# Feed forward in units of two, four, four, four and two tiles, and another order of the steps

## The chip, the core and the metric

The kernel runs on one core of a Trainium2 chip. The metric is the device time of one execution in microseconds (us), the median of three runs. A core has five engines with queues of their own: TensorE (PE in the profile) for matmuls, with its weight loads shown apart (PEld), VectorE (DVE), ScalarE (ACT), GpSimd (POOL) and SyncE (SP), which issues nearly all DMAs here.

## The reference, cut to what matters

One transformer block over 2048 rows of 640 bf16 numbers: linear attention with 32 heads of 20, then a feed forward layer of width 1728.

```python
x = A_x                                    # 1 x 2048 x 640
h = x + attention(layernorm(x), wqkv, w_phi, wo)
out = h + silu(layernorm(h) @ w1) @ w2     # w1: 640 x 1728, w2: 1728 x 640

# attention, for each head, on q, k, v of 20 columns:
phi(a) = concat(softmax(a @ w_phi), softmax(-(a @ w_phi)))     # 40 features
kv, z  = sum over rows of phi(k)^T v,  sum over rows of phi(k)
o      = phi(q) @ kv / (phi(q) @ z + 1e-6)
attention = concat of the heads' o @ wo
```

The sums kv and z run over all 2048 rows, so no query can be used before the last key has been added.

## The kernel before, in words

The rows are cut into 16 tiles of 128 (T = 16). The kernel is a dictionary of small steps, each a Python function that emits a few instructions, and a string ORDER that lists the steps' names. The program is emitted in exactly that order, so ORDER fixes the order on every engine's queue: an engine runs its own instructions in the order of the string and waits at each for its inputs and for its buffer. A second table, ON, says which engine takes some of the copies and normalisations.

The steps, with a tile's number t, and the line at which the profile shows them:

- `WKc`, `WVc`, `Xa`, `loadi`, `wph`: loads of weights and input on SP (L163, L166, L490). `X2` brings tiles 2 and 3. `load0` is wo, `load1` to `load5` the five row blocks of w1, `load6` to `load9` four parts of w2, `load10` and `load11` its last 64 rows.
- `wk`, `wke`, `fk`, `fke` (TensorE L292, L316, copies L309, L325): w_phi folded into the key weights at the start; `wq` (a transposing DMA, L388), `fq`, `fqe` (L400, L406) the same for the query weights. `own`, `phq`, `phi_a`, `phi_b`, `ones`, `pad`, `mask`, `eqp` prepare constants.
- `st t` (VectorE L434, L435), `rs t` (GpSimd L443, L446 or ScalarE L440), `xn t` (VectorE or GpSimd L450): the first layernorm. `xt t` transposes the tile: tiles 0 to 3 on TensorE (L457, copied by `x t`, L477), the others by a DMA that SP issues (L479).
- `K t`, `V t` (TensorE L498; tile 0's V in five parts, L510), `ex t` (ScalarE L539), `su t` (VectorE L543), `rk t` (ScalarE L551, L552), `sc t` (VectorE L556), `ve t` (ScalarE L560), `kv t` (TensorE L575): keys' features, values and their sums. `bd0`, `bd1` (VectorE L584, L586) turn the sums into block diagonal weights.
- `Q t` (TensorE L522), `qe t` (ScalarE L639), `qs t` (VectorE L643), `qr t` (VectorE L651, L653, L661), `qt t` (a transposing DMA, L667): queries' features.
- `D t` (TensorE L692), `E t0`, `E t1` (VectorE L704, L705), `ot t` (transposing DMA, L716), `G t0`, `G t1` (TensorE L725), `ga t0`, `ga t1` (VectorE L732): numerator and denominator, division, output projection, residual.
- `ls t` (L434, L435), `lr t` (GpSimd L443, L446), `hn t` (VectorE L450), `ht t` (transposing DMA, L752): the second layernorm, transposed into the buffer HnT.
- Feed forward by units of tiles, a unit named by its first tile a: `ua.f` (TensorE L815) multiplies column chunks of w1 from f on (128 columns each, 13 whole chunks) with the unit's HnT, into one PSUM bank of 512 numbers; `sa.f` (ScalarE L835) takes silu of the bank into shT. The last 64 columns of w1 go the other way round (`ua.L`, L826; `sa.L`, L841; `lta`, a transposing DMA, L845). `d t0`, `d t1` (TensorE L853, L856) multiply with w2, `oa t0`, `oa t1` (VectorE L862) add the residual, `out t` (L867) stores.

Before the change the units are tile 0, tile 1, and then pairs (2, 3) to (14, 15). A unit of n tiles has a moving operand of 128 n columns, so 128 in the first two units and 256 in the others. A piece, one bank, is four chunks in a unit of one tile and two in a unit of two. A unit's first `u` needs HnT of all its tiles. HnT has four buffers (NHN) of two tiles' size, shT three (NSH).

PSUM has eight banks. At first they are used as three pairs, with two banks for the sums over keys; from the step `halves` on as a ring of eight single banks, taken in turn, so that each use waits for the emptying of the one eight before it.

Of the kernel before, what the change touches and what calls it, by code (L numbers as in the profile page):

```python
# [15 lines left out]


ORDER = """
warm0 warm1 warm2 warm3 warm4 warm5 warm6 warm7 warm8 warm9 warm10 warm11 warm12 warm13 warm14 own pad0
X0 st0 phi_a WK0 WK1 wk0 warm15 warm16 warm17 WK2 wk1 rs0 xn0 WK3 WK4 xt0 warm18 wk2 X1 wke0 ones5 WV0  # L20
WV1 WV2 phi_b wk3 wke1 wke3 wk4 fk3 x0 WV3 wke2 WV4 fk2 wke4 st1 ones3 X2 fk1 fk3e fk4 rs1 fk1e fk2e X4
xn1 V0.0 st2 fk4e wph0 mask fk0 mask0 wph1 rs2 X8 V0.1 st3 xn2 V0.2 ones0 st4 fk0e phq xt1 ones1 x1 K0
ex0 rs3 V0.3 xn3 V1 zeros xt2 ve1 st6 x2 rs4 xn4 wq2 load10 rs6 xt4 K1 st5 su0 rs5 ex1 xt3 V2 ve2 K2 x3
ex2 rk0 wq0 V0.4 K3 fq2 ex3 xn5 xn6 V3 ve0 st8 fq2e su1 ones4 st7 ve3 wq3 ones2 rk1 sc0 V4 su2 ve4 rs7
xt5 fq0 xn7 load8 fq0e sc1 kv0 st9 su3 K4 xt6 wq4 fq3 rs8 ex4 rk2 st11 sc2 fq3e wq1 V5 rs9 kv1 ve5 st10
K5 rk3 K6 ex5 kv2 sc3 V6 ex6 xn8 fq1 ve6 xt7 xn9 xt8 rs10 pad1 kv3 su4 rk4 rs11 K7 su5 fq1e ex7 xn10 V7
fq4 rk5 ve7 wq5 sc4 kv4 su6 rk6 V8 sc5 st12 st14 st13 K8 kv5 xn11 fq4e ve8 ex8 xt9 xt10 ones6 fq5 fq5e
sc6 su7 K9 Q0 ex9 ones7 V9 load11 xt11 rk7 load7 qe0 kv6 rs12 K10 su9 sc7 xn12 su8 rs13 K11 load9 load1
rk9 ve9 rs14 xn14 st15 ex10 sc9 kv7 xn13 rk8 sc8 xt12 Q1 V10 ex11 qe1 ve10 su11 kv8 kv9 xt13 rk11 qs0
rs15 eqp K12 ex12 V11 su10 xn15 rk10 ve11 V13 K13 sc11 su12 ve13 xt14 sc10 V12 load5 ex13 kv10 qr0 kv11  # L30
su13 K14 V14 qs1 load2 xt15 qr1 rk13 ve12 load6 K15 load3 ex14 ve14 rk12 Q2 ex15 V15 su14 sc13 rk14 qe2
qt0 su15 Q3 sc14 Q4 sc12 rk15 ve15 kv12 kv13 qe3 sc15 mask1 kv14 qs2 qs3 Q5 qe4 qr2 kv15 qt1 qr3 bd1 bd0
Q6 load0 qe5 Q7 Q8 qe6 halves qt2 D0 qe7 qs4 qt3 Q9 E00 qe8 qe9 E01 D1 Q11 E10 E11 Q10 qr4 qe11 qe10 D2
qs5 ot0 Q13 qe13 G00 E20 G01 ot1 E21 ga00 ga01 ls0 D3 qt4 Q12 Q14 ot2 G10 qe12 E30 lr0 load4 hn0 E31 qs6
qr6 Q15 G11 G20 qe14 qr5 qe15 G21 ht0 ot3 ga11 ga10 u0.L ls1 lr1 ga20 u0.4 s0.L qt5 lt0 D4 E40 u0.12 hn1
u0.0 ga21 s0.0 u0.8 qs9 s0.12 ht1 qt6 G30 G31 s0.4 ga30 s0.8 d00 ga31 ls2 d01 E41 D5 u1.L u1.0 lr2 ls3
u1.4 oa00 s1.0 s1.L oa01 u1.8 u1.12 ot4 hn2 E50 s1.12 ht2 G40 lr3 hn3 ht3 E51 D6 qs7 s1.4 E60 G41 ga40
ot5 qr9 u2.0 s1.8 u2.10 E61 u2.2 u2.L qr7 ga41 s2.0 qs8 ls4 u2.6 u2.12 G50 s2.10 lt1 s2.2 lr4 G51 qr8
hn4 s2.L ga51 u2.4 s2.4 ot6 lt2 u2.8 ga50 ls5 s2.8 lr5 qs10 hn5 qs12 qt7 s2.6 qr10 d11 d10 s2.12 qt8 ht4
G60 ht5 oa10 out0 D7 d31 ga60 qs15 d30 E70 qt9 d20 E71 oa11 oa20 out1 G61 ot7 u4.0 oa30 D8 oa31 u4.8  # L40
s4.0 qr12 d21 qt10 u4.L ga61 s4.8 E80 E81 s4.L ls6 u4.12 oa21 qs11 qr15 s4.12 u4.2 D9 u4.6 s4.2 lr6 u4.4
G70 u4.10 E90 s4.4 lt4 hn6 G71 s4.10 ot8 E91 out2 G80 s4.6 ot9 G81 ga71 ga81 ga70 d50 d41 G90 ls7 qs13
lr7 ht6 hn7 D10 oa50 ga80 ls8 ht7 lr8 E100 out3 hn8 d40 G91 d51 qr11 oa40 E101 oa41 u6.0 ga91 ga90 u6.12
oa51 qr13 ot10 u6.10 u6.6 u6.L s6.L s6.0 s6.6 u6.2 u6.4 qt11 lt6 s6.12 ls9 s6.10 u6.8 G100 lr9 s6.4 s6.2
ht8 s6.8 hn9 ht9 out5 D11 G101 qs14 d60 u8.L out4 s8.L d61 ga101 E110 ga100 u8.0 qt12 qr14 u8.10 s8.0
oa60 E111 ot11 qt15 ls10 d70 oa61 G110 lt8 D12 oa70 G111 E120 u8.4 qt13 lr10 s8.10 u8.8 u8.6 E121 qt14
u8.12 s8.8 ga110 D13 s8.4 ga111 ls11 E130 lr11 hn10 u8.2 s8.12 s8.6 d71 oa71 hn11 ot12 out7 ht11 s8.2
E131 d90 out6 d80 G120 d91 G121 oa80 ga120 ht10 ot13 u10.0 oa90 oa91 ga121 s10.0 D14 u10.4 E140 u10.L
u10.12 E141 G130 u10.8 s10.4 D15 ga130 s10.12 s10.8 ls12 u10.2 E150 u10.10 lr12 s10.L G131 E151 hn12
ot14 u10.6 G140 d81 ga131 s10.2 lt10 G141 out9 oa81 out8 ls13 s10.10 s10.6 ht12 ga140 lr13 d110 ga141  # L50
hn13 d101 d100 ls14 ht13 d111 oa110 u12.0 u12.2 u12.10 oa100 ot15 oa111 u12.4 oa101 u12.L u12.12 s12.0
s12.2 s12.4 u12.8 lr14 s12.10 u12.6 hn14 s12.L G150 s12.8 s12.6 s12.12 G151 ht14 ga150 lt12 out10 out11
d120 ga151 ls15 lr15 d121 oa120 hn15 ht15 d130 oa121 out12 u14.L oa130 u14.0 s14.L lt14 u14.2 s14.0
u14.4 s14.2 u14.6 s14.4 u14.8 s14.6 u14.10 s14.8 u14.12 s14.10 d131 s14.12 d140 oa131 out13 d141 oa140
d150 oa141 out14 d151 oa150 out150 d152 oa151 out151 oa152 out152
""".split()

# [2 lines left out]
def kernel(  # L60
# [82 lines left out]

    ON = dict(
        rs0="ACT", xn0="DVE", wke0="DVE", wke1="DVE", wke3="ACT", x0="DVE", wke2="DVE", wke4="DVE",
        fk3e="ACT", rs1="POOL", fk1e="DVE", fk2e="ACT", xn1="DVE", fk4e="ACT", rs2="POOL", xn2="DVE",
        fk0e="ACT", x1="ACT", rs3="ACT", xn3="DVE", x2="ACT", rs4="ACT", xn4="DVE", rs6="POOL", rs5="POOL",
        x3="ACT", xn5="POOL", xn6="POOL", fq2e="ACT", rs7="POOL", xn7="POOL", fq0e="ACT", rs8="ACT",
        fq3e="ACT", rs9="ACT", xn8="POOL", xn9="POOL", rs10="ACT", rs11="POOL", fq1e="ACT", xn10="POOL",
        xn11="POOL", fq4e="ACT", fq5e="ACT", rs12="POOL", xn12="POOL", rs13="POOL", rs14="POOL", xn14="DVE",  # L150
        xn13="POOL", rs15="ACT", xn15="POOL",
    )


# [614 lines left out]
    def ffn_step(at):  # L769

        u = unit(int(at))
        steps = [f"u{u[0]}.{p[0]}" for p in pieces(u)]
        downs = [f"d{t}{g}" for t in range(*u) for g in range(2)]
        k = 2 * (at - u[0]) / (u[1] - u[0])
        return steps[int(k * len(steps))] if k < 1 else downs[int((k - 1) * len(downs))]
# [70 lines left out]

    def ffn_down(u, t, g):
        k, n = t - u[0], (u[1] - u[0]) * P
        ps = ps_of["d", t, g] = ps_half()
        a, b = groups(t)[g]  # L850
        for fc in range(FC - 1):
            at = fc * n + k * P
            nc.tensor.matmul(  # L853
                ps[:, 0 : b - a], shT[u][:, at : at + P], w2_sb[:, fc, a:b], start=(fc == 0), stop=False,
            )
# [74 lines left out]
```

## Time and profile before

| what | us |
|---|---|
| median of three runs (238.47, 239.26, 239.35) | 239.26 |
| the profiled execution | 239.66 |
| its span, from the first instruction to the last | 237.9 |
| TensorE busy in the span | 229.7 |
| VectorE busy | 170.5 |
| ScalarE busy | 104.4 |
| GpSimd busy | 55.2 |
| first matmul of D0, from the span's start | 76.1 |
| first matmul of the last step with matmuls (d152) | 233.1 |

The profile is of one execution, and all times below count from the start of its span. A matmul's row is longer than its share of the stream, since matmuls overlap in the array; what a matmul costs is read from one start to the next. TensorE's granted clock was 0.997 of full speed over the span, and full from 4.3 us on.

### The profile page before, as it was taken

What the parts mean: (1) busy time and instruction counts of PE and PEld (TensorE: products, weight loads), DVE (VectorE), ACT (ScalarE), POOL (GpSimd) and SP (SyncE); (2) the same over time, 40 slices, a digit from 0 to 9 for tenths busy, and PEclk for the clock granted to TensorE, in tenths of its full rate; (3) what the DMA queues carried; (4) which work ended last, traced back from release to release, by engine and by line L of the source; (5) the groups of instructions that cost most, each with busy time, mean ns of one, the idle gap of its engine ahead of it and who ended that gap; (6) DMA issues with size and microseconds to landing.
All of it is one profiled execution on the core that took longest, in us unless ns stands there. A gap on an engine that the chain in (4) does not pass through costs nothing.

```text
span 237.9 us, 5586 instructions
## 1 busy us (share of the span) xinstructions
PE 229.7 (97%) x2253; PEld 180.4 (76%) x2253; DVE 170.5 (72%) x355; ACT 104.4 (44%) x222; POOL 55.2 (23%) x99
## 2 busy tenths in 40 slices
PE   7999999989999999999999999999999999999993
...
DVE  4799999999999999979997869854535634242021
...
PEclk9999999999999999999999999999999999999998
...
GB/s 170 295 282 125 126 156 62 283 179 87 230 184 64 145 155 102 110 98 39 149 118 116 62 56 56 96 167 85 165 51 90 36 54 83 30 61 63 0 46 38
DMA packets 67472, 26.87 MB, mean 113 GB/s; under 512 B 60407, under 2 KB 66423, under 8 KB 67319
## 3 DMA queue, kind: packets, MB, share of 16 engines
...
q14 instruction: 8, 0.07, 0.1%
...
## 4 chain that ended last, share of the span: by engine, by line
PE 75%; POOL 9%; DMA 7%; DVE 3%; ACT 2%; issue 1%; SPq 1%; POOLq 0%; DVEq 0%
PE banks L815 23%; PE banks L853 23%; PE banks L725 9%; PE banks L522 8%; POOL xn L450 7%; PE banks L498 5%; DMA X<-in_A_x_dram 2%; PE banks L692 2%; DMA OT<-O 2%; PE banks L856 2%; DVE st L434 2%; DMA Wk<-in_A_wqkv_dram 2%; DMA w_sb<-in_B_w_dram 1%; PE banks L575 1%; PE banks L826 1%
## 5 line engine op out<-in xcount | busy, mean ns | idle before, releaser
L835 ACT ACTIVATE shT<-banks 128x512 bf16<-128x512 f32 (+2 forms) x57 | 30.1, 560 | 75.3 <-PE banks L815 75.2
L853 PE MATMUL banks<-w_sb,shT 128*128 128x320 bf16 (+2 forms) x429 | 61.4, 295 | 0.0
L815 PE MATMUL banks<-HnT,w_sb 128*128 128x256 bf16 (+1 forms) x585 | 61.0, 261 | 0.0
L815 PEld LDWEIGHTS <-w_sb 128*128 128x128 bf16 x585 | 51.0, 98 | 5.5
L853 PEld LDWEIGHTS <-shT 128*128 128x128 bf16 x429 | 41.1, 98 | 14.9
L443 POOL TENSOR_SCALAR rs<-mv 128x1 f32<-128x1 f32 x25 | 5.7, 228 | 149.8 <-DVE mv L435 149.8
L862 DVE TENSOR_TENSOR o_t<-banks,X 128x320 bf16<-128x320 f32 (+2 forms) x33 | 15.5, 476 | 33.3 <-PE banks L856 28.0
L498 PEld LDWEIGHTS <-XnT 128*128 128x128 bf16 x310 | 29.4, 98 | 11.8 <-DMA XnT<-xn 1.2
L434 DVE BATCH_NORM_STATS2 st<-X 128x6 f32<-128x320 bf16 x64 | 27.9, 478 | 5.1 <-DMA X<-in_A_x_dram 4.9
L450 POOL TENSOR_SCALAR xn<-X,mv,rs 128x640 bf16<-128x640 bf16 x10 | 25.3, 2532 | 5.5 <-ACT rs L441 5.2
L725 PE MATMUL banks<-wo_sb,OT 128*128 128x320 bf16 x160 | 25.6, 299 | 0.2 <-DMA OT<-O 0.2
L732 DVE TENSOR_TENSOR X<-banks,X 128x320 bf16<-128x320 f32 x32 | 14.8, 481 | 15.2 <-PE banks L725 15.2
L498 PE MATMUL banks<-Wfk,XnT 128*128 128x320 bf16 x160 | 24.2, 299 | 0.8 <-DMA XnT<-xn 0.8
L643 DVE TENSOR_REDUCE Sq<-EQ 128x66 f32<-128x1320 bf16 x16 | 24.1, 1512 | 0.0
L522 PE MATMUL banks<-Wfq,XnT 128*128 128x360 bf16 (+2 forms) x160 | 23.6, 299 | 0.0
L639 ACT ACTIVATE EQ<-banks 128x660 bf16<-128x660 f32 (+2 forms) x46 | 21.8, 558 | 3.9 <-PE banks L522 3.7
L543 DVE TENSOR_REDUCE Sk<-EK 128x64 f32<-128x1280 bf16 x16 | 23.3, 1468 | 0.0
L498 PE MATMUL banks<-Wv,XnT 128*128 128x320 bf16 x150 | 22.5, 299 | 0.0
L539 ACT ACTIVATE EK<-banks 128x640 bf16<-128x640 f32 x32 | 20.7, 698 | 3.2 <-PE banks L498 2.2
L522 PEld LDWEIGHTS <-XnT 128*128 128x128 bf16 x160 | 15.1, 97 | 6.1
L725 PEld LDWEIGHTS <-OT 128*128 128x128 bf16 x160 | 15.3, 98 | 5.8 <-DMA OT<-O 0.5
L705 DVE TENSOR_TENSOR O<-banks,Rd 128x360 bf16<-128x360 f32 (+1 forms) x32 | 15.7, 491 | 1.1
...
## 6 DMA issues: line engine op xcount, KB each, us to landing
...
```

The source lines that it names most:

```text
L434: nc.vector.bn_stats(st[:, i, :], X[:, t, i * HD : (i + 1) * HD])
L450: eng.tensor_scalar(out=xn_[t][:], in0=X[:, t, :], scalar1=mv_.pop(t)[:, 0:1], scalar2=rs_.pop(t)[:], op0=ALU.subtract, op1=ALU.mult,)
L498: nc.tensor.matmul(ps[:, g, 0:HD], XnT[:, c, t * P : (t + 1) * P], W[:, c, g * HD : (g + 1) * HD], start=(c == 0), stop=(c == C - 1),)
L522: nc.tensor.matmul(ps[:, 0 : e - a], XnT[:, c, t * P : (t + 1) * P], Wfq[:, c, a:e], start=(c == 0), stop=(c == C - 1),)
L539: nc.scalar.activation(E5[:, :, :, b, :], p4, AF.Exp, scale=sign)
L543: nc.vector.tensor_reduce(sk[t][:], ek[t][:, 0 : H * HF].rearrange("p (q f) -> p q f", f=DH), axis=AX.X, op=ALU.add)
L639: nc.scalar.activation(features(t, a, b)[:, :, :, i], p4, AF.Exp, scale=sign)
L643: nc.vector.tensor_reduce(sq[t][:], EQ[0][:, t, :, 0:FCH].rearrange("p c (q f) -> p c q f", f=DH), axis=AX.X, op=ALU.add)
L725: nc.tensor.matmul(ps[:, 0:HD], ot[t][:, c, :], wo_sb[:, c, g * HD : (g + 1) * HD], start=(c == 0), stop=(c == C - 1),)
L815: nc.tensor.matmul(ps[:, at : at + n], w1_sb[:, c, fc * P : fc * P + P], HnT[u][:, c, 0:n], start=(c == 0), stop=(c == C - 1),)
L835: nc.scalar.activation(shT[u][:, f0 * n : f1 * n], ps_of.pop(("u", u, f0))[:, 0 : (f1 - f0) * n], AF.Silu)
L853: nc.tensor.matmul(ps[:, 0 : b - a], shT[u][:, at : at + P], w2_sb[:, fc, a:b], start=(fc == 0), stop=False,)
```

## The change

The units become (0, 1), (2 to 5), (6 to 9), (10 to 13) and (14, 15). The moving operand has 256 columns in the first and the last unit and 512 in the three between; a piece there is one chunk. HnT and shT hold four tiles, with three and two buffers. `ua.L` does each tile once (before, a unit of one tile did it twice to fill the 128 rows), and its transpose and w2's last rows follow the tile's number in the unit. An unused helper (`ffn_step`) goes, and there are twenty matmuls ahead of the kernel's work instead of nineteen (WARM).

ORDER is another one from its start up to the last unit's steps; it holds the same steps, but for the units' pieces and `warm19`. ON gives the normalisations of tiles 4 and 14 (`xn4`, `xn14`) to GpSimd, which then has twelve of them instead of ten, and moves `wke0`, `wke1`, `x0` from VectorE to ScalarE, `rs0`, `rs3`, `rs9`, `rs10` to GpSimd and `rs6`, `rs7`, `rs11` to ScalarE. Between the last `kv` and `D0` stands one Q instead of three, so that ten Q follow D0 instead of seven. SP issues the twelve loads ahead of `X2` in the same order as before; `load9` now stands between `xt7` and `xt8`, `load10` between `lt0` and `qt7`.

```diff
-    WARM = 19
+    WARM = 20
...
-    NHN = 4
-    NSH = 3
-    SINGLE = 2
+    NHN = 3
+    NSH = 2
...
-        xn11="POOL", fq4e="ACT", fq5e="ACT", rs12="POOL", xn12="POOL", rs13="POOL", rs14="POOL", xn14="DVE",
-        xn13="POOL", rs15="ACT", xn15="POOL",
+        wke0="ACT", rs0="POOL", wke1="ACT", xn0="DVE", wke3="ACT", wke2="DVE", fk3e="ACT", rs1="POOL",
+        x0="ACT", wke4="DVE", xn1="DVE", fk2e="ACT", fk1e="DVE", fk0e="ACT", fk4e="ACT", x1="ACT",
+        rs2="POOL", xn2="DVE", rs3="POOL", x2="ACT", xn3="DVE", rs4="ACT", x3="ACT", rs6="ACT", xn4="POOL",
...
-    UNITS = [(t, t + 1) for t in range(SINGLE)] + [(t, t + 2) for t in range(SINGLE, T, 2)]
+    UNITS = [(0, 2)] + [(t, t + 4) for t in range(2, T - 2, 4)] + [(T - 2, T)]
...
-            HnT[u] = persist.tile([P, C, 2 * P], BF16, name="HnT", bufs=NHN)
+            HnT[u] = persist.tile([P, C, 4 * P], BF16, name="HnT", bufs=NHN)
...
-        m = 2 if u[1] - u[0] == 2 else 4
+        m = 4 // (u[1] - u[0])
...
-        for j in range(2):
+        for j in range(n // P):
...
-                    ps[:, j * FL : (j + 1) * FL], HnT[u][:, c, (j * P) % n : (j * P) % n + P],
+                    ps[:, j * FL : (j + 1) * FL], HnT[u][:, c, j * P : (j + 1) * P],
...
-            shT[u] = pools["late"].tile([P, 2 * (FC - 1) * P], BF16, name="shT", bufs=NSH)
+            shT[u] = pools["late"].tile([P, 4 * (FC - 1) * P], BF16, name="shT", bufs=NSH)
...
-        nc.tensor.matmul(ps[:, 0 : b - a], shT_l[u][:, 0], w2_last[:, k, a:b], start=False, stop=True)
+        nc.tensor.matmul(ps[:, 0 : b - a], shT_l[u][:, k // 2], w2_last[:, k % 2, a:b], start=False, stop=True)
```

Of ORDER, the stretch around D0 and the one around the first units, before and after:

```diff
-qt0 su15 Q3 sc14 Q4 sc12 rk15 ve15 kv12 kv13 qe3 sc15 mask1 kv14 qs2 qs3 Q5 qe4 qr2 kv15 qt1 qr3 bd1 bd0
-Q6 load0 qe5 Q7 Q8 qe6 halves qt2 D0 qe7 qs4 qt3 Q9 E00 qe8 qe9 E01 D1 Q11 E10 E11 Q10 qr4 qe11 qe10 D2
...
+V15 qe2 kv12 Q5 rk14 su15 qs2 sc14 qe3 rk15 kv13 sc15 kv14 ve15 qt0 kv15 qe5 load1 qr2 Q7 halves bd0 bd1
+qt1 qs3 D0 E00 Q4 E01 D1 qe7 qe4 qr3 Q9 E10 qe9 Q6 qt2 load3 Q8 E11 qe6 Q10 D2 ot0 G00 qe8 qs5 pad0 qs4
+qr4 E20 qt3 G01 E21 ot1 Q11 ga01 qr5 ga00 qe10 Q14 qt4 G10 qe11 D3 ls0 ot2 qt5 ga10 E30 E31 G11 qe14 Q12
+ga11 D4 lr0 Q13 hn0 ls1 G20 qe12 E40 qe13 ot3 lr1 hn1 ga20 Q15 G21 ht0 qe15 E41 G30 D5 G31 ht1 u0.0 u0.2
...
+lr5 s0.12 d01 ga41 d00 hn5 ls4 lr4 qs8 ht2 hn4 qs10 qr8 ot6 oa00 d11 oa01 ht5 ht4 D7 d10 G60 E70 oa10
+out0 G61 u2.6 E71 qt8 u2.0 oa11 qr10 u2.9 u2.11 ga61 s2.0 s2.6 ga60 s2.9 s2.11 qs9 qr9 u2.2 D8 u2.L ot7
```

More of the change, by code (lines that the diff above doesn't have):

```diff
@@ L18 @@
 ORDER = """
[L19 to L28, printed above, removed]
@@ L34 @@
[L34 to L38, printed above, removed]
@@ L44 @@
[L44 to L53, printed above, removed]
@@ L54 @@
-u14.4 s14.2 u14.6 s14.4 u14.8 s14.6 u14.10 s14.8 u14.12 s14.10 d131 s14.12 d140 oa131 out13 d141 oa140
+warm0 warm1 warm2 warm3 warm4 warm5 warm6 warm7 warm8 warm9 warm10 warm11 warm12 warm13 warm14 phi_b
+phi_a ones1 X0 WK0 WK1 WK2 st0 wk0 warm15 warm16 warm17 warm18 WK3 wk1 warm19 WK4 wke0 rs0 X1 WV0 WV1
+WV2 wke1 wk2 wk3 xn0 wke3 fk3 WV3 xt0 wke2 WV4 fk2 fk3e X2 st1 wk4 wph1 X4 rs1 fk1 wph0 x0 wke4 xn1 fk0
+fk2e wq2 zeros fk1e fk4 V0.0 V0.1 xt1 ones6 fk0e own fk4e st2 x1 rs2 st3 K0 xn2 ex0 X8 K1 st4 V0.2 ones3
@@ new lines @@
+rs3 V0.3 wq3 xt2 ex1 x2 xn3 su0 V1 xt3 K2 rs4 ve1 x3 rk0 V0.4 K3 st6 st5 V3 st7 ones0 ex2 sc0 phq fq2
+rs6 xn4 ex3 V2 ve3 fq3 ve0 su1 xt4 st8 fq2e load11 rs7 ve2 rs5 wq0 xn5 kv0 xt5 su2 xn6 rk1 V4 sc1 K4
+ones2 fq3e fq0 ve4 kv1 wq1 V5 rs8 ex4 xt6 wq4 K5 xn7 su3 rk2 xt7 st10 xn8 fq0e fq1 ve5 sc2 st9 rk3 rs9
+kv2 K6 ex5 su4 sc3 fq1e load9 st11 K7 xn9 kv3 st12 st13 rs10 rk4 sc4 ones4 ex6 ex7 xt8 V6 xn10 xt9 wq5
+fq4 su5 V7 ve6 fq4e V8 ve7 ones7 su6 ones5 rk5 rs12 st15 rs11 V9 rs13 xn11 ve8 sc5 K8 load2 kv4 ve9 rk6
@@ new lines @@
+fq5 ex8 fq5e xt10 su7 rk7 sc6 su8 xn13 K9 st14 kv5 Q0 load6 xt11 rs15 K10 sc7 load4 ex9 su9 xn12 qe0 kv6
+Q1 kv7 xt13 mask eqp rs14 ex10 xn14 rk8 qs0 sc8 rk9 su10 V10 K11 qe1 xt12 V11 ve10 sc9 ex11 rk10 su11
+V13 qs1 ve11 rk11 kv8 sc11 load0 K12 sc10 qr0 xn15 K13 ve13 kv9 xt14 ex12 load7 K14 ex13 su12 su13 mask0
+kv10 V14 kv11 xt15 load5 rk12 ex14 sc12 rk13 ve14 V12 mask1 K15 su14 sc13 load8 ve12 Q2 Q3 pad1 qr1 ex15
+V15 qe2 kv12 Q5 rk14 su15 qs2 sc14 qe3 rk15 kv13 sc15 kv14 ve15 qt0 kv15 qe5 load1 qr2 Q7 halves bd0 bd1
@@ new lines @@
+qt1 qs3 D0 E00 Q4 E01 D1 qe7 qe4 qr3 Q9 E10 qe9 Q6 qt2 load3 Q8 E11 qe6 Q10 D2 ot0 G00 qe8 qs5 pad0 qs4
+qr4 E20 qt3 G01 E21 ot1 Q11 ga01 qr5 ga00 qe10 Q14 qt4 G10 qe11 D3 ls0 ot2 qt5 ga10 E30 E31 G11 qe14 Q12
+ga11 D4 lr0 Q13 hn0 ls1 G20 qe12 E40 qe13 ot3 lr1 hn1 ga20 Q15 G21 ht0 qe15 E41 G30 D5 G31 ht1 u0.0 u0.2
+qs6 u0.4 E50 ot4 ga21 ga30 u0.10 E51 u0.L ot5 ga31 qr6 s0.0 G40 s0.L u0.8 ls3 qt6 qs7 G50 qr7 s0.2 u0.6
+ls2 lt0 ga50 s0.10 s0.4 lr3 s0.6 G51 ga40 lr2 u0.12 G41 D6 load10 hn3 qt7 ga51 hn2 ls5 E60 s0.8 ht3 E61
@@ new lines @@
+lr8 ht6 ot11 ga90 d50 d40 qs15 ls9 oa30 lr9 ht7 oa21 hn8 oa31 G100 hn9 out2 qs14 oa40 d51 G101 ht9 ht8
+G110 out3 G111 ga110 ga111 d41 ga100 oa50 u6.L D12 oa51 u6.0 qr14 s6.L ga101 E120 u6.11 qt13 u6.1 s6.0
+s6.1 oa41 E121 u6.8 D13 u6.12 ls10 E130 ls11 lr11 s6.12 E131 u6.2 s6.11 ot12 qt14 u6.10 u6.5 out4 u6.9
+s6.8 u6.6 u6.3 ot13 qr15 u6.4 s6.5 s6.2 s6.3 s6.9 qt15 G120 s6.4 u6.7 s6.10 lr10 G121 lt6 G130 ga120
+s6.6 G131 D14 ga121 s6.7 hn11 ga131 ga130 ht11 out5 ls13 d60 hn10 ls12 lr13 lr12 d61 oa60 d70 E140 d71
```

42 lines of the change are left out of this document (19 added, 23 removed).

## The prediction

> **What bounds the kernel now.** I read the engines' totals first, then the 40 slices.
>
> ```profile
> PE 229.7 (97%) x2253; PEld 180.4 (76%) x2253; DVE 170.5 (72%) x355; ACT 104.4 (44%) x222; POOL 55.2 (23%) x99
> ...
> PE   7999999989999999999999999999999999999993
> ...
> DVE  4799999999999999979997869854535634242021
> ...
> PEclk9999999999999999999999999999999999999998
> ```
>
> TensorE is busy in every slice and VectorE in nearly every one of the first 20 (5.9 us each), so both limit the first half and TensorE alone the second. A busy PE row may hide waits, so I then listed TensorE's matmuls in order of time and compared the distance from each step's first matmul to the next step's with its columns. From 5.5 us to the last step they add up but for eight gaps: 0.67 us before fk3, 0.15 and 0.12 beside it, 0.72 before xt2, 0.99 before K6, 0.94 before kv8, 0.18 before G30, 0.37 before G110. The chain of waits names some causes (columns: start, length, what):
>
> ```profile
> 6.44 5.68 DMA X<-in_A_x_dram
> 12.15 0.90 DVE st L434 x2
> ...
> 50.05 1.52 DVE EK L556 x2
> 51.62 0.85 PE banks L575 x22
> ```
>
> X2 lands at 12.12 and st2 starts at once; xt2 follows at 14.78. Later sc9 and sc8 end just ahead of kv8. From 12.14 to 86.4 VectorE's rows lie end to end: it is a queue that never empties. Where it hands over, at bd0 and D0, TensorE starts 0.2 us behind it (VectorE's rows end at 75.90, D0 starts at 76.14, both by the instructions in order of time). So the start of D0 is set by VectorE's queue and its end by TensorE's work behind D0. That splits the sum in two.
>
> What slows VectorE I found by laying its rows beside GpSimd's:
>
> ```profile
> 41.93 0.80 DVE L556 TENSOR_TENSOR EK<-EK,Rk 128x1280 bf16<-128x1280 bf16 x1
> 45.44 1.30 DVE L556 TENSOR_TENSOR EK<-EK,Rk 128x1280 bf16<-128x1280 bf16 x1
> ```
>
> ```profile
> 40.97 2.51 POOL L450 TENSOR_SCALAR xn<-X,mv,rs 128x640 bf16<-128x640 bf16 x1
> 45.19 2.52 POOL L450 TENSOR_SCALAR xn<-X,mv,rs 128x640 bf16<-128x640 bf16 x1
> ```
>
> sc6, begun 0.96 us into an xn of GpSimd, took 0.80; sc7, begun 0.25 into one, took 1.30. Of the eight sc that met a busy GpSimd (sc0 to sc7) four were long (1.14 to 1.33).
>
> **Up to D0.** From st2 on I add what each VectorE step takes from its start to the next step's (st and ls 1.04, xn 0.39, su 1.40, sc undisturbed 0.735, qs 1.44, qr 1.07, both bd 1.28). Before: 14 st 14.57, 4 xn 1.56, 16 su 22.34, 16 sc 11.76, 4 qs 5.75, 4 qr 4.29, bd 1.28, sum 61.55; from 12.14 that ends at 73.69, and the queue was really there at 75.76. The 2.07 between are the four long sc (0.33 to 0.52 each) and xn14 (1.04 for 0.39). After: 14 st, 2 xn, 16 su, 16 sc, 3 qs, 3 qr, both bd: 14.57 + 0.78 + 22.34 + 11.76 + 4.31 + 3.22 + 1.28 = 58.26. X2 keeps its place in SP's queue behind the same twelve loads, so st2 again starts at 12.14; what VectorE does ahead of it (wke0, wke1 and x0 go to ScalarE) fits into its idle 1.7 us there. Sum 70.40 plus disturbance. GpSimd now takes twelve xn instead of ten, so eleven sc (sc0 to sc10) can meet one: at four in eight, 5.5 x 0.43 = 2.4; if only starts in an xn's first 0.7 us of 2.48 are hit, 3 x 0.43 = 1.3. I take 1.9; the ends are 0.5 (one hit) and 5.5 (eleven at 0.5). bd1 ends at 72.3, **D0 starts at 72.35**, 3.8 earlier than before.
>
> The Trainium skill (SBUF — State Buffer, "Who interferes with whom") says that a VectorE instruction with two SBUF inputs contends with a GpSimd instruction that reads SBUF, and that the one that issues second blocks fully until the first is done. The rows above bear out the contention and not its size: sc6 ran in 0.80 inside an xn.
>
> TensorE must be there by then. K0 comes at some 11.4, since fk4e is now the last of five copies of 0.69 on ScalarE (before: 11.07), and xt2 at 14.78 as before, since X2, st2, rs2 and xn2 stand as they did. From xt2 to D0 it has 16 V 20.64, 14 K 19.01, 6 Q 8.20, 16 kv 5.47, folds and transposes 2.00: 55.32, so 70.1 without a wait. Two waits are likely. GpSimd's row of xn starts at about 17.6 (rs2 at 13.4 as before, then rs3 and phq, 0.9 and 1.7) and with 2.48 each and the rs between ends xn7 at 28.9; SP issues xt7 in 1.2 and it lands at 31.7, against K7 at 31.3 (16.5 of work behind xt2): 0.4. And load9 (640 KB) now stands in SP's queue ahead of xt8. The row for that is load8 before (480 KB): issued behind xt5, it landed 4.8 us after it, and xt6 behind it at 30.26, 5.7 after its issue, where the median is 2.8; that was the 0.99 before K6. Behind xt7 at 31.7 that puts xt8 at 37.1 (load 4.8, itself 0.6) against V8 at 36.4: 0.7, with ends of 0 and 2.3 (the load longer by its size). So 71.2; D0 waits for VectorE, and these waits cost nothing while they stay under 2.2 in all. That cover is gone if VectorE turns out quick (rival 1). The other ten xt have 0.3 to 3 us to spare by the same sums.
>
> **Behind D0.** For the widths I use the chain's rows:
>
> ```profile
> 91.60 1.12 PE banks L815 x20
> ...
> 202.66 4.37 PE banks L815 x40
> ...
> 211.41 1.77 PE banks L853 x13
> ```
>
> 128 columns cost 0.0560 us, 256 0.1092, 320 0.1358: a line of 0.416 ns a column and 2.6 ns a matmul. 512 columns are not in the trace; the line gives 0.2156, two of 256 0.2185. I take the line, as three rows lie on it. Feed forward up, before: 130 x 0.0560 + 455 x 0.1092 + 90 x 0.029 (L826) = 59.6. After: 130 x 0.1092 + 195 x 0.2156 + 80 x 0.029 = 58.6. **Minus 1.0** (minus 0.4 with 0.2185). All else is the same work in another order. From D0 to the last step d152, before: 16 D 5.47, 7 Q 9.56, 32 G 21.73, up 59.56, down 60.12, sum 156.4. After, three more Q stand behind D0: 5.47 + 13.66 + 21.73 + 58.61 + 60.12 = 159.6.
>
> The Trainium skill (TensorE: Matmul & The Clock Gate, "Back-to-back issue gap") gives N/2.4 + 2.5 ns, with which these rows agree, but also sustained spacings of 81 ns at 128 columns and 131 at 512; the row here is 56 at 128. With 131 the 195 matmuls would lose another 16.5 us (rival 4).
>
> Waits behind D0, before: 0.18 and 0.37. After, I looked for steps whose producer ends late. ga00 frees a bank for D3 at about the moment D3 comes up: 0 to 0.1. u0.0 needs both ht0 and ht1: hn1 ends 18.2 of VectorE's work after bd1 plus some 0.4 for lr1 (GpSimd, 0.9), at 90.9, and ht1 takes 1.2 to issue and lands 2.5 later: 93.4, against u0.0 at 72.35 + 21.14 = 93.5. I take 0.2. u2.6, the first four-tile unit, needs ht4: VectorE has 36.9 behind bd1, and between 76 and 101 us of before it fell 0.8 behind its sum: 110.0, landing 112.7, against 72.35 + 40.9 + 0.3 = 113.5. I take 0.2 for it and 0.1 for D3. Later VectorE has less than TensorE: its sum up to hn9 is 9.5 less than TensorE's up to u6.L, up to hn12 21 less than up to u10.1. Half a microsecond, as before (0.55).
>
> Hidden: silu of a 512 bank takes 0.60 and TensorE needs 1.08 to fill one; the two-buffer shT and three-buffer HnT are free some 40 us ahead; load10, late now, has 4 us before d01's last matmul; the twentieth warm matmul lies in the wait for WK1. The tail behind d152 is the same.
>
> **Sum.** D0 3.8 earlier, work behind it 3.15 more, waits equal: minus 0.65. The profiled execution took 239.66 (span 237.9), 0.4 over the median of 239.26; from its own time 239.0, from the median **238.6**. Half a per cent, 1.2 us, is about what a measurement of this kernel can tell from no change.
>
> **Rivals.** (1) *VectorE is disturbed less.* One sc hit: D0 is set by TensorE at 71.2, 1.2 earlier: 237.4; if xt8 is on time too, 236.7. For it: two of the long ones came in one run of back-to-back xn, which may be chance. Against: more xn. 0.32. (2) *The first four-tile unit waits for its last tile*, slower: TensorE cannot start u2.6 before ht4, while a unit of two needed only ht2 and ht3. Its margin is 0.8; each microsecond that VectorE lags beyond goes into the time, and from a lag of 2.7 on the kernel is over 0.5% slower. With 3.5: 241.3. For it: VectorE lay 2 us further behind its sum at ga40 than at D0 before. Against: 1.1 of these it waited for TensorE. 0.13. (3) *Disturbed more:* all eleven sc long, D0 at 75.9: 242.2. 0.07. (4) *Wide matmuls overlap:* were one of 512 no dearer than the 320 row, 195 x 0.080 = 15.6 less: 223. The line through three widths speaks against it, the sustained figures of the page on TensorE for it. 0.01. (5) *Full blocking:* each of eleven sc waits half an xn, 1.24, so 13.6 instead of 1.9: 250.3. This is the rule of the page on SBUF; sc0, sc2 and sc6 speak against it. 0.02. That the wide matmul saves nothing is in the forecast's range (239.2).
>
> **How the numbers follow.** Forecast 0.45, own range 238.1 to 240.3, all within 0.5%. Faster: rivals 1 and 4, 0.33. Slower: 2, 3 and 5, 0.22. The range 236.7 to 241.3 leaves out the upper half of rivals 2 and 3, and 4 and 5, some 0.15.
>
> **What would show it.** st2 at 12.1; bd1's end near 72.3 and D0 at once behind it; sc of 1.1 to 1.3 beside starts of xn; 0.216 a matmul in L815's rows of 512; no gap over 0.5 behind D0. Wrong it would be made by st2 starting elsewhere, gaps on VectorE between 12 and 72 us, or a wait of TensorE behind D0 that I have not listed.

## The result and the profile after

| | before | after |
|---|---|---|
| median, us (six runs each) | 238.92 | 237.67 |
| range, us | 238.46 to 239.35 | 237.39 to 238.16 |
| ratio to before, 95% interval | | 0.9945 [0.9924, 0.9965] |
| the profiled execution, us | 239.66 | 237.69 |
| its span | 237.9 | 235.7 |
| st2 starts on VectorE | 12.14 | 11.00 |
| VectorE's last row of bd0 and bd1 ends | 75.90 | 72.24 |
| first matmul of D0 | 76.14 | 71.72 |
| first matmul of d152, the last step | 233.09 | 232.07 |
| last store issued, and landed | 234.47, 236.87 | 233.37, 234.81 |

The kernel became 1.25 us faster, 0.55%. The forecast was 0.65 us and "within 0.5%". The measured 237.67 lies just past that bound: below the forecast's own range (238.1 to 240.3), inside the whole range (236.7 to 241.3). The two profiled executions differ by 1.97: 1.02 up to the start of d152, the rest behind it. Busy time and slices of the kernel after:

```profile
PE 230.1 (98%) x1984; PEld 160.9 (68%) x1984; DVE 167.0 (71%) x350; ACT 104.2 (44%) x221; POOL 63.6 (27%) x103
...
PE   8899999999999999999999999999999999999995
...
DVE  3799999999999999999998997672482320422021
```

TensorE is as full as before, with 269 matmuls fewer, and VectorE waits only 0.9 in all between 11 and 72 us. TensorE's waits after 20 us, by line:

```profile
PE banks L496 <- DMA XnT<-xn: 0.8, 2, 0.4
PE banks L690 <- DVE KVB L584: 0.2, 1, 0.2
PE banks L723 <- DMA OT<-O: 0.2, 1, 0.2
```

L496 is K and V: two waits for a transposed tile (ahead of K7 and V8). L690 is D0, which waits for bd1 (L584) in its middle. L723 is G30. In order of time, from the chain of waits:

```profile
70.86 0.56 DVE KVB L582
...
72.02 0.23 DVE KVB L584
...
72.30 0.30 PE banks L690 x5
...
87.75 4.08 DMA OT<-O
...
152.46 4.32 PE banks L805 x20
```

D0's second half starts 0.05 behind the end of VectorE's bd1, so VectorE's queue still sets D0. Twenty matmuls of 512 columns took 4.32, which is 0.216 each.

### The profile page after: what moved, and what is told of

It reads as the page before. It is cut to its first block, busy times and chain, and to the rows that moved or that the text cites. A ratio compares the mean times of both kernels' runs of the same rounds, so it can differ in the third digit from the quotient of the medians.

```text
span 235.7 us, 5028 instructions
## 1 busy us (share of the span) xinstructions
PE 230.1 (98%) x1984; PEld 160.9 (68%) x1984; DVE 167.0 (71%) x350; ACT 104.2 (44%) x221; POOL 63.6 (27%) x103
## 4 chain that ended last, share of the span: by engine, by line
PE 82%; DVE 5%; DMA 4%; ACT 4%; POOL 2%; issue 2%
PE banks L845 24%; PE banks L805 24%; PE banks L723 9%; PE banks L496 8%; PE banks L520 6%; DMA XnT<-xn 2%; POOL xn L448 2%; PE banks L690 2%; PE banks L215 2%; PE banks L848 2%; DMA OT<-O 2%; DVE EK L554 2%; DVE Sk L541 1%; ACT EK L537 1%; PE banks L314 1%
## 5 line engine op out<-in xcount | busy, mean ns | idle before, releaser
L825 ACT ACTIVATE shT<-banks 128x512 bf16<-128x512 f32 (+1 forms) x53 | 28.6, 592 | 72.3 <-PE banks L805 71.1
L805 PE MATMUL banks<-HnT,w_sb 128*128 128x512 bf16 (+1 forms) x325 | 59.4, 336 | 0.0
L805 PEld LDWEIGHTS <-w_sb 128*128 128x128 bf16 x325 | 31.3, 98 | 22.4 <-DMA HnT<-xn 0.2
L441 POOL TENSOR_SCALAR rs<-mv 128x1 f32<-128x1 f32 x26 | 7.3, 279 | 137.2 <-DVE mv L433 137.2
L496 PEld LDWEIGHTS <-XnT 128*128 128x128 bf16 x310 | 29.2, 98 | 12.2 <-DMA XnT<-xn 1.4
L448 POOL TENSOR_SCALAR xn<-X,mv,rs 128x640 bf16<-128x640 bf16 x12 | 31.0, 2593 | 1.5 <-ACT rs L439 1.2
L723 PE MATMUL banks<-wo_sb,OT 128*128 128x320 bf16 x160 | 25.5, 299 | 0.2 <-DMA OT<-O 0.2
L637 ACT ACTIVATE EQ<-banks 128x360 bf16<-128x360 f32 (+2 forms) x52 | 22.2, 512 | 6.0 <-PE banks L520 5.9
L496 PE MATMUL banks<-Wfk,XnT 128*128 128x320 bf16 x160 | 24.0, 299 | 0.5 <-DMA XnT<-xn 0.4
L496 PE MATMUL banks<-Wv,XnT 128*128 128x320 bf16 x150 | 22.5, 299 | 0.4 <-DMA XnT<-xn 0.4
L723 PEld LDWEIGHTS <-OT 128*128 128x128 bf16 x160 | 15.1, 98 | 6.9 <-DMA OT<-O 0.5
```

The lines of the kernel that those rows point to most:

```text
L448: eng.tensor_scalar(out=xn_[t][:], in0=X[:, t, :], scalar1=mv_.pop(t)[:, 0:1], scalar2=rs_.pop(t)[:], op0=ALU.subtract, op1=ALU.mult,)
L496: nc.tensor.matmul(ps[:, g, 0:HD], XnT[:, c, t * P : (t + 1) * P], W[:, c, g * HD : (g + 1) * HD], start=(c == 0), stop=(c == C - 1),)
L637: nc.scalar.activation(features(t, a, b)[:, :, :, i], p4, AF.Exp, scale=sign)
L723: nc.tensor.matmul(ps[:, 0:HD], ot[t][:, c, :], wo_sb[:, c, g * HD : (g + 1) * HD], start=(c == 0), stop=(c == C - 1),)
L805: nc.tensor.matmul(ps[:, at : at + n], w1_sb[:, c, fc * P : fc * P + P], HnT[u][:, c, 0:n], start=(c == 0), stop=(c == C - 1),)
L825: nc.scalar.activation(shT[u][:, f0 * n : f1 * n], ps_of.pop(("u", u, f0))[:, 0 : (f1 - f0) * n], AF.Silu)
```

## The experiments

Each kernel ran on one chip beside the kernel before (median 239.04 to 239.16 there). "After" is the kernel after the change; times of single steps are from the profiles, counted as above; D0 and u0.0 stand for their first matmuls. u0.0 is the first up matmul of after.

| run | ratio to before, 95% interval | bd1 ends | D0 | u0.0 |
|---|---|---|---|---|
| after | 0.9945 [0.9924, 0.9965] | 72.24 | 71.72 | 93.64 |
| n256 | 0.9969 [0.9953, 0.9984] | 71.80 | 71.28 | 93.44 |
| n128 | 1.0024 [1.0002, 1.0046] | 72.65 | 72.13 | 94.15 |
| cover | 1.0004 [0.9986, 1.0023] | 73.49 | 74.25 | 95.12 |
| best1 | 1.0017 [0.9992, 1.0042] | 74.56 | 75.33 | 96.03 |
| xnv | 1.0043 [1.0022, 1.0064] | 74.20 | 73.68 | 96.29 |
| cover2 | 0.9924 [0.9896, 0.9952] | 72.24 | 73.44 | 94.03 |
| dist | 0.9928 [0.9894, 0.9962] | 72.02 | 71.87 | 93.44 |
| best2 | 0.9933 [0.9906, 0.9959] | 71.62 | 72.83 | 93.37 |
| x2b | 0.9963 [0.9945, 0.9980] | 74.88 | 75.13 | 92.16 |

In cover, best1, cover2 and best2 Q4 (1.37) stands ahead of D0 instead of behind it, so their D0 is not to be compared with that of after; their u0.0 is. x2b is in the order of before, where other steps stand ahead of u0.0; its D0 and u0.0 are to be set beside 76.14 and 93.17 of before.

### The width: n256 and n128

```diff
-            for c in range(C):
-                nc.tensor.matmul(ps[:, at : at + n], ..., HnT[u][:, c, 0:n], ...)
+            for e in range(0, n, 256):
+                for c in range(C):
+                    nc.tensor.matmul(ps[:, at + e : at + e + 256], ..., HnT[u][:, c, e : e + 256], ...)
```

n128 has 128 in place of 256.

> The changed kernel with each matmul of 512 columns given as two of 256 into the same bank; order, units, buffers and everything else unchanged. Theory (the whole net gain is the smaller fixed cost of wide matmuls; TensorE is the limit behind u0): 195 x (2 x 0.1092 - 0.2158) = +0.5 us against the changed kernel, so about 238.2 against its 237.67, ratio to the kernel before about 0.997. Rival (the order made the gain, the width nothing): 237.7, ratio 0.9945 unchanged. A second rival (two matmuls of 256 wait for their weights, which were loaded once for 512): over +2 us.

> The changed kernel with every up matmul cut to 128 columns: four for each of 512, two for each of 256 in the first and last unit. Theory (a fixed cost of 2.6 ns a matmul, nothing else): 195 x (4 x 0.0560 - 0.2158) + 130 x (2 x 0.0560 - 0.1092) = 1.6 + 0.4 = +2.0 us, so about 239.7, ratio to the kernel before about 1.003. Rival (weight loads of 98 ns a matmul come to the surface at 128 columns): +195 x 0.18 = some +35 us. Rival (width does nothing): 237.7.

n256 took 238.23, n128 239.53. From 512 to 256 columns the ratio rises by 0.0024, 0.57 us; from 512 to 128 by 0.0079, 1.9 us. By the line of the prediction (2.6 ns a matmul and 0.416 a column) it is 195 x 2.9 ns = 0.57, and 195 x 8.4 ns + 130 x 2.8 ns = 2.0. Both lie at their theories. The intervals of after and n256 overlap, so the 0.57 alone is not clear of noise, and the rival of no change is not out by the time; the 1.9 of n128 is clear of it, far from both of its rivals. The same step (u6.11, u6.1 and so on) in n256, from the chain of waits:

```profile
152.43 4.37 PE banks L806 x40
```

Forty matmuls of 256 columns took 4.37, against 4.32 for twenty of 512: 2.5 ns for each of 512. So the width is worth 0.5 to 0.6 us over two matmuls of 256, and what is left of n256's gain, 0.0031 or 0.74 us, belongs to the rest of the change. That rest still holds some width: units 0 and 1 have 65 matmuls of 256 instead of 130 of 128, and L826 has ten matmuls fewer, which by the prediction's prices is 0.2 and 0.3.

### Where load9 stands, and a cover for D0: cover and cover2

```diff
-xt6 wq4 K5 ... xt7 ... fq1e load9 ... xt8 V6 xn10 xt9 wq5 ... fq5e xt10
+xt6 K5 ... xt7 wq4 ... fq1e ... xt8 V6 xn10 xt9 load9 wq5 ... fq5e xt10
...
-Q7 halves bd0 bd1 qt1 qs3 D0 E00 Q4
+Q7 Q4 halves bd0 bd1 qt1 qs3 D0 E00
```

This is cover. In cover2 load9 stands behind xt10, so behind wq5 too.

> The changed kernel with three steps moved so that TensorE's waits up to D0 go: wq4 behind xt7 on SP (the wait before K7, 0.52), load9 behind xt9 (before V8, 0.56), Q4 ahead of D0 (the wait inside D0, 0.41). Theory (VectorE sets the pace up to u0.0, whose ht1 landed at 93.59 against a start at 93.64): the 1.5 us appear again as a wait of TensorE ahead of G30 or u0.0, and the time stays at 237.7 within 0.3, ratio 0.994 to 0.995. Rival (TensorE's waits simply add up): 236.2, ratio 0.988.

> The kernel after, with wq4 behind xt7, load9 behind xt10 (so ahead of no transpose and no query weight that is soon needed) and Q4 ahead of D0. Against the run cover the only difference is that load9 no longer stands ahead of wq5 in SP's queue. Theory (cover lost its 1.4 us to fq5, which waited 1.8 us for wq5): the wait behind kv4 is gone, and the time falls back to that of the kernel after, ratio 0.9945, or 0.1 us below it, since the first up matmul waits for ht1, which VectorE's queue sets, whatever TensorE does ahead of it. Rival A (TensorE's sum sets the time): the waits ahead of K7 and V8 are gone and Q4 fills the one at D0, 1.2 us less than after, ratio 0.9895. Rival B (Q4 ahead of D0 is what costs): ratio 1.000 as in cover, D0 at 74.

cover took 239.14, 1.4 us more than after: neither theory had that. Its longest wait of TensorE, and the same in its chain:

```profile
PE banks L398 <- DMA WTq<-in_A_wqkv_dram: 1.8, 1, 1.8
```

```profile
36.92 5.93 DMA WTq<-in_A_wqkv_dram
...
42.90 0.29 PE banks L398 x5
```

L398 is fq5, which needs wq5. wq5 was issued right behind load9 and took 5.93 to land, where it took 4.48 in after and 2.9 in cover2 (36.70 to 39.61). K9 stands behind fq5, ex9 and su9 behind K9, so VectorE waited as well, and bd1 ended 1.25 later than in after. I had moved a 640 KB load from ahead of xt8, where TensorE waits 0.56, to ahead of wq5, where it waits 1.8.

In cover2 that wait is gone and the time is 237.47, as the theory had it; rival B falls. The waits ahead of K7 and V8 are gone, and Q4 fills the one at D0, yet bd1 ends at 72.24 as in after and u0.0 starts 0.4 later. TensorE saved nothing: it waits 0.5 ahead of V9 and 1.3 ahead of K14 instead, so that its waits from 12 us through D0 are 1.78 in all, against 1.73 in after. Its waits, and its chain of waits around K14:

```profile
PE banks L496 <- DMA XnT<-xn: 1.5, 2, 1.1
```

```profile
51.73 2.83 POOL xn L448
...
54.58 3.15 DMA XnT<-xn
...
57.73 0.05 issue
57.77 1.53 PE banks L496 x10
```

K14 needs xt14. SP issued it at 54.58 (54.65 in after), when GpSimd had ended xn14, and it landed at 57.73 (57.02 in after, where K14 started at 57.07). GpSimd's rows lie end to end from 41.7, with the memsets of mask and EQ, 1.6 us, ahead of xn14. From K14 to D0 the chain has no row of VectorE. So here a third queue, GpSimd's, held TensorE, which neither theory nor rival A had: that VectorE's queue alone takes up what TensorE saves is not shown, and rival A, whose premise did not come about, is not tried by this run.

### Contention between GpSimd and VectorE: xnv and dist

```diff
-        ... xn4="POOL", xn5="POOL", ... xn15="POOL"
+        ... xn4="DVE", xn5="DVE", ... xn15="DVE"
```

> The kernel after, with the twelve normalisations of GpSimd (xn4 to xn15) on VectorE. Theory (VectorE's queue sets D0, and GpSimd's disturbance of it is what the profile of after shows row by row): VectorE gets 12 x 0.39 = 4.7 us more and loses some 1.9 us of stretching, so D0 comes 2.7 us later: 2.7 us slower than the kernel after, ratio to before 1.006. Rival (the disturbance is larger than the rows show, as every row beside GpSimd is a little longer): ratio at or below 0.997. Second rival (TensorE sets D0): no change, ratio 0.9945.

xnv took 240.27. Ratio 1.0043 is 2.3 us over after, where 2.7 was expected; bd1 and D0 came 1.96 later, and the rivals fall. Counted as in the prediction, against undisturbed durations, VectorE's queue from st2 to bd1 had 0.16 us of disturbance instead of 2.85 in after, so taking the twelve normalisations off GpSimd gave back 2.7 of the 4.7 that they cost on VectorE. The theory holds: work added to VectorE's queue comes out at D0, and the disturbance is what its rows show.

Which rows these are, in after. First VectorE, then GpSimd, in order of time (start, length, operation):

```profile
14.53 1.20 DVE L448 TENSOR_SCALAR xn<-X,mv,rs 128x640 bf16<-128x640 bf16 x1
...
57.19 0.63 DVE L651 TENSOR_TENSOR Rho<-Sq,Rq 128x66 bf16<-128x66 f32 x1
57.85 0.99 DVE L659 TENSOR_TENSOR EQ<-EQ,Rho 128x660 bf16<-128x660 bf16 x1
```

```profile
14.36 1.19 POOL L367 TENSOR_TENSOR phi_q<-WPQ,own_q 120x600 bf16<-120x600 bf16 x1
...
25.85 5.54 POOL L448 TENSOR_SCALAR xn<-X,mv,rs 128x640 bf16<-128x640 bf16 x2
...
57.06 1.46 POOL L239 TENSOR_SCALAR_AFFINE_SELECT mask<-mask 128x378 f32<-128x378 f32 x2
```

xn3 took 1.20 beside phq (VectorE's other xn 0.44 to 0.45); the last two rows of qr0, 0.23 and 0.50 elsewhere, took 0.63 and 0.99 beside the masks. Together 1.6 of the 2.85; the rest is in five smaller ones (sc1 and su11 lost 0.23 and 0.33 waiting for ScalarE, st10, st12 and sc6 were 0.16 to 0.44 too long). The sc steps, which carried the forecast's disturbance, ran in 0.77 to 0.83 but for sc6 (0.97); it was GpSimd's xn that stretched beside them, where they began while an sc was under way (xn8 3.05, xn14 2.81, xn5 2.64; the other nine 2.50 to 2.53).

```diff
-ex2 sc0 phq fq2 ... mask0 kv10 ... mask1 ... pad1 ... pad0
+ex2 sc0 ones4 ones5 ones7 phq fq2 ... pad1 pad0 mask0 kv10 ... mask1
```

> The kernel after, with three memsets of GpSimd (ones4, ones5, ones7) ahead of phq and the two pads ahead of mask0. In the profile of after xn3 on VectorE took 1.13 for 0.39 beside phq, and qr0 1.96 for 1.07 beside mask0. Theory (the stretch comes from these two GpSimd instructions, and VectorE's queue sets D0 until TensorE does): xn3 takes 0.4 and qr0 1.1, bd1 ends 1.6 earlier, D0 0.4 earlier, where TensorE's own sum stops the gain, and the wait ahead of G30 goes: 0.75 us less than after, ratio 0.9915. Rival A (the stretch only moves to other rows): ratio 0.9945. Rival B (VectorE alone counts): 1.6 less, ratio 0.988.

dist took 237.53. VectorE and GpSimd in it:

```profile
14.56 1.47 DVE L448 TENSOR_SCALAR xn<-X,mv,rs 128x640 bf16<-128x640 bf16 x1
...
57.69 0.23 DVE L651 TENSOR_TENSOR Rho<-Sq,Rq 128x66 bf16<-128x66 f32 x1
58.06 0.50 DVE L659 TENSOR_TENSOR EQ<-EQ,Rho 128x660 bf16<-128x660 bf16 x1
```

```profile
14.60 1.25 POOL L367 TENSOR_TENSOR phi_q<-WPQ,own_q 120x600 bf16<-120x600 bf16 x1
...
57.49 1.30 POOL L235 MEMSET w_last<- 64x640 bf16 x2
58.87 1.47 POOL L239 TENSOR_SCALAR_AFFINE_SELECT mask<-mask 128x378 f32<-128x378 f32 x2
```

Half of it worked. qr0 is undisturbed beside memsets, 0.9 us won. xn3 got worse: the memsets were done early and phq, 0.24 later than in after, ended later. In all nine profiles with the order of after or close to it, xn3 ends 0.18 behind phq's end, whichever of them began first. And most of what was won was lost again: V5 waited 1.2 for xt5 in this execution, the keys' exponentials came later, and VectorE waited 0.33 for ex8 and 0.31 for ex11 (0.25 for ex11 alone in after). bd1 ended only 0.2 earlier. The gain over after, 0.14 us, is less than the interval; this is the expectation's rival A in effect, though not by its mechanism.

### The landing of X2: x2b, again_b

x2b is the kernel before with one step moved; again_b is the kernel before itself, for another profile.

```diff
-X1 wke0 ones5 WV0
-WV1 WV2 ... st1 ones3 X2 fk1
+X1 wke0 ones5 WV0
+X2 WV1 WV2 ... st1 ones3 fk1
```

> The kernel before, with X2 four loads earlier in SP's queue, ahead of WV1. Theory (VectorE's queue begins when X2 lands and sets D0): X2 lands some 1 to 1.7 us earlier, st2 starts by 11.2 instead of 12.1, and what is gained there is in the time: 0.5 to 1 us less than before, ratio 0.996 to 0.998. Rival (the landing of the first loads differs by a microsecond from one execution to the next, and the profiled execution of before was a late one): st2 hardly moves in the mean, ratio 1.000, with a wide spread of the single times.

> The kernel before, unchanged, in another execution. In its first profile X2 landed at 12.12, and in the profiles of six kernels with the order of after or close to it at 10.63 to 11.05, behind the same twelve loads. Theory (the landing of the first loads varies from one execution to the next, and the first profile of before had a pause of 1.3 between the loads): X2 lands near 10.9, st2 starts at 11.0, D0 near 75.1 and the profiled time is near 238.7. Rival (something in the order of before holds the loads up): X2 lands at 12.1 again, D0 at 76.1, time near 239.6.

again_b took 239.41. X2 landed at 12.50, st2 started at 12.52 and D0 at 76.51: not the theory's chance but the rival. Its chain of waits:

```profile
6.45 6.05 DMA X<-in_A_x_dram
12.50 0.02 issue
12.52 0.90 DVE st L434 x2
```

With the order of before ahead of it X2 landed at 12.12, 12.50, 11.72 and 11.44 (the last two in wide_old2 and wide_old, below); with the order of after, behind the same twelve loads, in seven profiles at 10.63 to 11.05. What differs in SP's queue around it is what follows: in before X4 (640 KB) is issued right behind X2, at 6.92; in after a load of a few KB (wph1) stands between, and X4 comes at 7.51. Each load is spread over 16 DMA engines and has landed when the last is done. In again_b 15 parts of X2 had landed by 11.39 and the last one did at 12.50; in after by 10.48 and 10.83. That X4's parts are what held up the last one was not tried.

x2b took 238.42, 0.6 us less than before (0.9 by the ratio). X2 landed at 9.19, st2 started at 10.33, D0 at 75.13, 1.0 to 1.4 earlier than in the two profiles of before. So this start matters in before, and half of it or more reached the time.

### Everything together: best1 and best2

best1 is cover with X2 ahead of WV1 and D5 ahead of G30; best2 is cover2 and dist with X2 ahead of WV1.

> As the run with the three moves, and X2's load four places earlier in SP's queue (ahead of WV1), and D5 ahead of G30. Theory (VectorE's queue starts when X2 lands, and sets the pace up to u0.0): st2 starts about 1 us earlier, ht1 lands about 1 us earlier, u0.0 starts near 92.6, and the time is 236.6, ratio 0.990. Rival (X2 does not matter, since VectorE's early steps or GpSimd's hold it up as well): as the run with three moves. Rival (TensorE's waits add up): 236.0 or less.

> The edits of cover2 and of dist together, and X2 ahead of WV1 as in x2b. Theory (the queue of VectorE up to hn1 and the sum of TensorE up to the first up matmul are within half a microsecond of each other in after, so only what shortens both counts): VectorE 0.7 earlier at st2 and 1.6 less stretched, TensorE 0.7 earlier at xt2 and 1.1 less of waits ahead of K7 and V8, with Q4 in the wait at D0: the first up matmul 1.6 us earlier, ratio 0.988, 236.1 us. Rival (the landing of the weights WV1 to WV4, 0.4 us later each, holds TensorE ahead of xt2, and the gains do not add): ratio 0.992 as in cover2.

best1 took 239.79: it has cover's wait for wq5. It does not try the earlier X2: X1 landed at 8.58 in it and at 7.45 in best2, behind the same loads, and the steps of VectorE behind X1 came so late that st2 started at 11.83, with X2 there at 9.87. best2 took 237.53, no better than cover2 or dist. X2 landed at 9.22 in it, and st2 still started at 10.91, against 11.00 in after. The reason stands in VectorE's rows of after:

```profile
10.27 0.81 DVE L323 CAST Wfk<-banks 128x640 bf16<-128x640 f32 x1
11.01 0.88 DVE L432 BATCH_NORM_STATS2 st<-X 128x6 f32<-128x320 bf16 x2
```

In the order of after st2 stands behind fk1e, which ends when st2 starts; X2 is no longer what it waits for. And with X2 ahead X4 landed 0.7 later, which st4 waited for. V5's wait for xt5 came here too (1.3). The gains did not add, as the rival had it. No version beats after by more than the intervals allow to tell.

### The units alone: wide_old and wide_old2

```diff
-... u4.0 ... u4.8 s4.0 ...
+... u2.0 u2.1 ... u2.8 u2.9 s2.0 s2.1 ...
...
-... d31 d30 d20 ... d21 ... d50 d41
+... d20 d21 oa20 oa21 out2 d30 d31 oa30 oa31 out3 d50 d41
```

> The four-tile units alone: the order, the table of engines and the warm-up of before, with the pieces of the new units at the places of the last old unit that they contain, and the second products of the earlier tiles moved directly ahead of those of the later tiles. Theory (the other order is there to make the wide units possible): between the old first up matmul of tiles 2 and 3 and that of tiles 4 and 5 TensorE loses 7.4 us of work that it used to do while VectorE finished tiles 4 and 5, and has little to put in its place, so it waits some 4 to 9 us: 243 to 248 us, ratio 1.017 to 1.037. Rival (only the width counts, the order is neutral): 1.0 us less of up matmuls, ratio 0.996.

> The four-tile units in the order of before, as in the run wide_old, with eleven emptying steps (silu of three pieces, two residuals of G and the divisions of tiles 5 and 9 among them) moved forward, so that no PSUM bank is refilled before it is emptied; in wide_old eleven banks were, so part of its silu and division worked on another step's sums. Theory (the time of wide_old is waits: each engine's fixed order was made for units of two, so TensorE waits for ht, these for VectorE's rows behind others that wait for TensorE): 265 to 285. Rival (the refilled banks caused most of the waits): 243 to 248, as first expected.

wide_old took 279.58 (ratio 1.1701 [1.1649, 1.1752]), but it leaves out the emptying of eleven PSUM banks before they are filled again, so part of its work is on another step's sums and its time is no measure of the units. wide_old2 empties them first and took 271.29 (one execution). TensorE's longest wait in wide_old2:

```profile
PE banks L805 <- DMA HnT<-xn: 8.9, 1, 8.9
```

The first expectation, 4 to 9 us, counted one wait, and there is one of 8.9: the first four-tile unit waits for its last transposed tile. But it does not stand alone: there are 7.2 in five waits for transposed O (L723) and 4.8 for an xn, and the granted clock was 0.968 over the span, against 0.999 in after. The theory, that an order made for units of two makes each engine wait for another in turn, agrees with the time (265 to 285 expected). The units cost 32 us with their pieces at these places; that no smaller change of the order would do was not tried.

## Why the prediction was right in its size, and where its steps failed

**Up to D0: right by luck, as two errors cancel.** The forecast had st2 at 12.14, 58.26 of work and 1.9 of disturbance, bd1's end at 72.3. Measured: st2 at 11.00, the same work, 2.85 of disturbance, 72.24. "X2 lands as before" failed: the loads ahead of it are the same, but it landed a microsecond earlier. Here the prediction's own sign of being wrong, st2 starting elsewhere, came true. "Eleven sc can be hit" failed as a mechanism: the sc were hardly touched; xn3 beside phq and qr0 beside the masks were.

The Trainium skill (SBUF — State Buffer, "Who interferes with whom") lists copy, cast and tensor_scalar of VectorE among those that can take the port pair shared with GpSimd, and says that the second to issue blocks fully. It also says that a VectorE instruction with two inputs in SBUF contends with a GpSimd instruction that reads SBUF, and not with one that only writes it. I had made the blocking rival 5 for the sc, where it fell again (0.77 to 0.83 beside xn). For xn3 and phq the trace agrees: xn3 ends 0.18 behind phq in nine profiles; and the last two rows of qr0 beside memsets took 0.23 and 0.50, undisturbed. That issue order decides the trace does not show: in dist xn3's row begins 0.04 ahead of phq's.

**D0 itself.** Forecast 72.35; the first six of its matmuls ran from 71.72 on bd0 alone, five waited until 72.30. The waits ahead of K7 and V8 were 0.52 and 0.56 (forecast 0.4 and 0.7). That they cost nothing agrees with cover2, but there K14's wait for xt14, behind GpSimd's queue, takes them up, a limit that the prediction did not list.

**Behind D0.** The work behind D0 was to grow by 3.15 with equal waits; from bd1's end to d152 it is 159.8 in after, against 157.2 before, 2.6 more (half of D0 now runs ahead of bd1's end). Width: 1.0 forecast for the whole; n128 confirms the line and n256 agrees with it. Waits behind D0: one, 0.33 ahead of G30 (ot3 issued at 87.74, landed at 91.82), where 0.5 was taken in three other places; a wait not listed was the other sign of being wrong, here of no weight. u0.0 started at 93.64, forecast 93.5, right behind ht1 (93.59); u2.6 at 113.40, forecast 113.5, with ht4 there at 111.98. So rival 2 fell, with 1.4 us to spare.

**The tail: "the same" was wrong by 1 us.** The last store took 2.40 from issue to landing in before and 1.44 in after. It is no chance: 2.10 in again_b, 2.38 in x2b, 1.73 in wide_old and 1.77 in wide_old2, all in the order of before, and 1.44 to 1.46 in after and every other kernel with its order. The DMA traffic of the last microseconds, before (234.0 to 236.2; columns: queue, kind, packets, MB, share; below, the last store's KB and time to landing):

```profile
q14 instruction: 1, 0.01, 0.9%
...
out_dram<-o_t SPq DMA_DIRECT2D x1, 32.0 KB, 2.4
```

and after (233.5 to 236.5, none of instructions):

```profile
q1 hardware_dynamic: 287, 0.08, 11.3%
...
out_dram<-o_t SPq DMA_DIRECT2D x1, 32.0 KB, 1.4
```

In before one packet of 8 KB of instructions is moved from 235.52 to 235.84, in the middle of that store. Fifteen of its 16 parts landed by 235.91, the last at 236.87. In after the next such packet comes at 237.5, when all is over. The same packet lies in the last store in x2b (233.83) and again_b (235.18), with one part some 0.9 and 0.6 behind the other fifteen. It lies there too in wide_old, with one part 0.27 late, and in wide_old2, where no single part is late (266.5 to 268.7):

```profile
q14 instruction: 1, 0.01, 0.9%
...
out_dram<-o_t SPq DMA_DIRECT2D x1, 32.0 KB, 1.8
```

So the packet goes with a late landing in five kernels, by 0.3 to 1.0. It isn't the number of all instructions that places it: n128 has 6454 rows of instructions and no such packet in its last store, wide_old2 has 5023 and one. It goes with VectorE's: the six kernels in which a packet of that kind comes in the last store or shortly ahead of it have 355 instructions of VectorE or, in xnv, 362 (there at 232.97, 3 us ahead of the last store, which took 1.45), and the eight others have 350. After has 350 because five copies and normalisations went from VectorE to ScalarE and GpSimd. That is read from counts, not tried.

The Trainium skill (DMA: Bandwidth & Descriptors, "Queues, rings and completion order") says that a DMA engine takes turns between its queues packet by packet; a late part on one engine alone agrees with that; wide_old2, where all parts are late alike, does not show it. I did not move the packet by itself, so the cause is read from the traces and not tried.

**The sum.** Forecast up to d152: minus 0.65; measured in the profiles, minus 1.02. Tail: forecast 0, measured minus 0.96 by the landing. Together that is about the 1.97 between the profiled executions, of which the medians show 1.25: the profiled execution of before was 0.7 over its median. That the total came out near the forecast is luck as well, since the tail, on which the forecast had nothing, is as large as all the rest. Rival 1 gave 237.4, near the result, but not by its mechanism: D0 was not set by TensorE. Rivals 3, 4 and 5 fell: D0 came at the forecast's time, and 512 columns cost 0.216.

So, counted in the two profiles, the 1.0 up to d152 is as much as the width was to give in all (0.6 over matmuls of 256, 0.5 in units 0 and 1 and L826): what the new order won ahead of D0 it paid behind it. The other 1.0 is the tail, where an instruction transfer no longer falls in the last store. How these two share the 1.25 of the medians is open.
